# Hgrn2 attention and a balanced expert layer on one core: the first expert's tokens taken after the second digit of the capacity search

## The chip, the cores and the metric

The kernel runs on one core of a Trainium2 chip. The metric is the device time of one execution in microseconds (us); less is better. The engines go by short names: PE is TensorE (its weight loads are PEld), DVE is VectorE, ACT is ScalarE, POOL is GpSimd, SP is SyncE. PE accumulates in PSUM, eight banks of 128 x 512 float32.

## The reference

Inputs q, k, v, f_logit have the shape (4, 8, 768, 48). Per batch and head a 48 x 48 state decays by a gate and takes up one outer product a step; its product with q is the output y:

```python
f = 1.0 / (1.0 + np.exp(-f_logit))
for t in range(S):
    state = f[:, :, t, :, None] * state + np.einsum('bhd,bhe->bhde', k[:, :, t], v[:, :, t])
    y[:, :, t] = np.einsum('bhd,bhde->bhe', q[:, :, t], state)
```

The result, laid out as x of 3072 tokens by 384, goes to 8 experts of equal capacity, 384 tokens each. All (token, expert) logits x @ w_gate are taken in falling order; a pair is granted if its token is free and its expert not full. Each expert then computes relu(x @ w1) @ w2 with w1 384 x 1024 and w2 1024 x 384, all float32.

## The kernel before

**Attention** works on 24 chunks (6 stretches of 128 steps, 4 batches) in a pipeline whose stages are listed by hand. For each chunk the rows x and the logits are stored in a DRAM tile xd, 480 numbers a row: 384 of x and copies of the 8 logits. The last stores are issued from ACT (store, L374 to L377), since SP's queue takes the weights.

**Search** (L624 to L650). Every token first wants the expert of its largest logit. The margin at which the fullest expert has 384 takers is found digit by digit, four digits of five bits. For each digit DVE writes above (is a token over a threshold), 24 small products count by expert, DVE takes the largest count and compares it with the capacity, and a product with unit turns that into a new base in PSUM bank A[1]. Beside these steps PE turns the last three chunks (turn_y), ACT copies them to x, POOL adds the logits, ACT stores them. At the end come idle products (idle_turns, L105), which write to a bank that nobody reads.

**Lists** (fast(), L926 on). Tokens over the final base are sure of their expert. `positions` gives each its place in the expert's list by two products and a scan over nine kinds (no expert, and eight experts); `numbers` and `sort` turn that into tables of token numbers with 24 products. This is done twice with one in_line table: first for the two blocks of expert 0, then for all 30 blocks. From the token numbers POOL issues indirect DMAs, in this order in its queue: two whole tiles x of expert 0 (L793); the logits lg of up to 6 x 128 tokens that are not placed (L962); then xe, four quarter tiles a tile of tokens, two tiles for each of the experts 1 to 4 (L799).

**Experts.** A tile is 128 tokens. `turn` brings it to xeT: by PE products Xe and a copy on DVE and one on ACT for expert 0 (L716 to L720), by DVE block transposes for the rest (L727). `up` makes H by 24 products a tile or group of tiles, in three PSUM banks taken in turn (tags Y, Y, L), ACT writes relu(H) to hT (L741); `down` makes O by 8 products a tile (L751), ACT copies it to one of three buffers o (L756), and POOL issues the scatter to the output by token number (L757). A float32 product shows as two PE instructions in the profile.

**Rounds.** The tokens not placed go through seven rounds of a search of their own (search_rest, products cnt, L850) on DVE and PE, while PE works through the first two tiles of NA = 5 experts. `pe_work` is the list of PE pieces with their costs; `clock` holds an estimate of the time of PE and DVE, and `PE(cost)` issues pieces until PE's estimate has caught up, so the order of PE's queue is fixed when the kernel is built. When the rounds end, the third tiles of the five experts follow, then the last three experts with three tiles each.

**Weights.** Each expert has 3 MB. There are five slots. Experts 0 and 1 are loaded by SP once y0 of the last chunk is there; the next are issued from within the expert two places ahead (L744); experts 5 to 7 go to the slots 0 to 2, after the third tiles. A one-element copy into the new tile (L584) sets the moment at which the load may start.

If an expert of the first five has fewer than 256 sure tokens (few), or another check strikes, a general path computes all again.

Of the kernel before, what the change touches and what calls it, by code (L numbers as in the profile page):

```python
# [25 lines left out]
def kernel(  # L26
# [315 lines left out]
    def turn_y(G):  # L342
        G["X"] = X = lengthy if G["i"] + B == len(chunks) else T[0]
        for hp in range(HP):
            nc.tensor.transpose(out=X[:, 128 * hp:128 * hp + 128], in_=G["yT"][:, hp, :],  # L345
                                identity=ident[:])
# [72 lines left out]
    NL = 6  # L419
    NQ = NL + TE * E  # L420
    NA = 5
# [75 lines left out]
    notfirst = const([128, KC, NT], FP16, "notfirst")  # L497
# [81 lines left out]
    def load_weights(e, pool, slot, parts=(0, 1), behind=None):  # L579
        for part in parts:  # L580
            shape, src = (([128, DC, F], moe_w1), ([128, FC, D], moe_w2))[part]
            w = pool.tile(shape, FP32, name=f"w{part + 1}", tag=f"w{part + 1}_{slot}", bufs=1)
            if behind is not None:
                (nc.gpsimd.tensor_copy if e < 2 else nc.scalar.copy)(  # L584
                    out=w[:, 0, 0:1], in_=behind)
# [37 lines left out]
    def search(over, choice, n):  # L623
        base = A[1][:, 128:129]  # L624
        for d in range(DIGITS):
            r = counts["r"]
            if d:
                above, r = rt([n, TH], f"above{n}", FP16), Y[d % 2]
                for h in range(2):
                    part = slice(n * h // 2, n * (h + 1) // 2)  # L630
                    stt(above[:, part], last_of(over[:, part], TH), base,
                        mid_of(steps[d][:], n // 2), ALU.subtract, ALU.is_ge)
                if d == 1:
                    gated(chunks[-1])
                    added0(chunks[-1])
                elif d == 2:
                    last_codes()
                for go in (turn_y, copy_y, with_logits, store):
                    go(chunks[d - DIGITS])
                for c in range(n):  # L640
                    nc.tensor.matmul(out=r[0:TH, 0:E], lhsT=above[:, c, :],
                                     rhs=choice[:, c, :], start=(c == 0), stop=(c == n - 1))
            most, filled = rt([1], "most"), rt([1], "filled", FP16)
            reduce(most[0:TH], r[0:TH, 0:E], ALU.max)
            ts(filled[0:TH], most[0:TH], CAP - 0.5, ALU.is_ge)
            nc.tensor.matmul(out=base, lhsT=units[d][0:TH, :], rhs=filled[0:TH],
                             start=(d == 0), stop=(d == DIGITS - 1), skip_group_check=True)
        idle_turns(3, Y[DIGITS % 2])
        return base
    def load_gate():  # L650
        for r in range(2):
            for a in range(2):
                nc.sync.dma_start(
                    out=wg_rows[DP * r:DP * r + DH, 2 * a:2 * a + 2],
                    in_=moe_w_gate.rearrange(
                        "(a r b d) e -> a r d b e", a=2, r=2, b=2)[a, r])
# [4 lines left out]
    with tc.manual_schedule(engines=FIXED):  # L661
# [7 lines left out]
        for e in range(2):  # L669
            load_weights(e, early, e, behind=chunks[-1]["y0"][:, 0, 0:1])  # L670
        base = search(over0[:], choice0, NT)
# [4 lines left out]
    def fast():  # L676
        stack = ExitStack()
        turns = {"H": cycle("YYL"), "O": cycle("A"), "r": cycle("T"), "b": cycle(["small"])}

        def bank(name, tag):  # L680
            return ps(name, next(turns[tag]))

# [3 lines left out]
        pe_work = deque()  # L686
        clock = {"pe": 0.0, "dve": 0.0}

        def V(n=1, cost=0.21):
            clock["dve"] += n * cost  # L690

        def PE(cost):
            while pe_work and clock["pe"] < clock["dve"] + 0.1:
                piece()
            clock["pe"] = max(clock["pe"], clock["dve"] + 0.1) + cost
            clock["dve"] = max(clock["dve"], clock["pe"] + 0.22)

        def piece():
            cost, go = pe_work.popleft()
            go()  # L700
            clock["pe"] += cost

        tiles = iter(range(NT))

        def ffn(e, first_block, n, ahead=None):
# [5 lines left out]
            def turn(i):  # L711
                def by_matmul():
# [6 lines left out]
                    nc.vector.tensor_copy(out=xT[:, 0, 0:128], in_=X[0][:, 0:128])  # L719
                    nc.scalar.copy(out=xT[:, 1:DC, 0:128],  # L720
# [10 lines left out]
                return (0.65, by_matmul) if e == 0 and first_block < 2 else (0.0, by_blocks)  # L731

            def up(ft, d):
                def go():
# [5 lines left out]
                    if d == DC - 1:  # L740
                        nc.scalar.activation(out=hT[:, ft, 0:w], in_=L["H"][:, 0:w], func=AF.Relu)  # L741
                        if ahead is not None and ft in (1, 6):
                            load_weights(ahead, pools[ahead], ahead, (ft // 6,),
# [46 lines left out]
        def fetch(e, i):  # L790
            if e == 0 and i < 2:
# [74 lines left out]
        def positions(kind, nk, n, code, notfirst_, held):  # L866

            incl = rt([nk, n], f"incl{n}", FP16)
            P = bank("P", "r")
            w = nk * n  # L870
            Pv = P[:, 0:w].rearrange("p (k c) -> p k c", c=n)
            PE(0.1)
            nc.tensor.matmul(out=Pv, lhsT=after16[:], rhs=kind[:], start=True, stop=False)
            nc.vector.tensor_tensor_scan(incl[:].rearrange("p k c -> p (k c)"), notfirst_,
                                         kind[:].rearrange("p k c -> p (k c)"), 0.0,
                                         op0=ALU.mult, op1=ALU.add)
            V(cost=0.1 + w / 350)
            PE(0.2)
            nc.tensor.matmul(out=Pv, lhsT=ones16[:], rhs=incl[:], start=False, stop=held is None)
            if held is not None:  # L880
                nc.tensor.matmul(out=Pv, lhsT=ones16[:], rhs=last_of(held, n), start=False,
                                 stop=True)
            sums = P[:, 256:256 + nk]
            total = rt([nk], f"total{n}", FP16)
            nc.vector.tensor_copy(out=total[:], in_=incl[:, :, n - 1])
            own, pos = rt([nk, n], f"own{n}"), rt([n], f"pos{n}")
            tt(own[:], Pv, kind[:], ALU.mult)
            reduce(pos[:], own[:].rearrange("p k c -> p c k"), ALU.max)
            q, line, blk = rt([n], f"q{n}"), rt([n], f"line{n}", FP16), rt([n], f"blk{n}", FP16)
            ts(q[:], pos[:], 0.5 - 64.0, ALU.add, 1.0 / 128.0, ALU.mult)  # L890
            ts(q[:], q[:], 12582912.0, ALU.add, -12582912.0, ALU.add)
            stt(line[:], q[:], -128.0, pos[:], ALU.mult, ALU.add)
            tt(blk[:], q[:], code, ALU.add)
            V(9)
            return total, line, blk

# [29 lines left out]
        with tc.manual_schedule(engines=engines):  # L926
            code = rt([NT], "code", FP16)
            stt(code[:], over0[:], base, code0[:], ALU.is_ge, ALU.mult)
            kind = rt([KC, NT], "kind", FP16, 1)
            tt(kind[:], mid_of(code[:], KC), kinds[:], ALU.is_equal)  # L930
            total, line, blk = positions(kind, KC, NT, code[:],
                                         notfirst[:].rearrange("p k c -> p (k c)"), None)
            idle_turns(11, "A")
            p0 = place_of(0, 0)
            r, in_line = sort(line, numbers(blk, value[:], blocks[:, p0:p0 + 2], NT, 2), NT, 2, 4)
            idle_turns(6, "A")
# [582 lines left out]
```

## Time and profile before

| | |
|---|---|
| median of 3 runs | 432.75 us (431.65 to 433.54) |
| the profiled execution | 431.0 us |
| its span on the core | 429.2 us |
| mean granted PE clock | 0.982 |
| PE busy | 410.2 us, 96% |
| DVE, ACT, POOL busy | 207.2, 149.5, 175.1 us |
| HBM read, written | 48.91 MB, 10.62 MB |

How to read it: the profile is of one execution. The span is what its engines' records cover. Times in the timeline are microseconds from the start of the span. A matmul record's length holds its way through the array as well, so lengths of products that follow each other overlap; the pitch of a row of them is read from the distance between the first and the next thing. The attention ends at about 137, the search at about 147.5, the lists at about 158; H of expert 0 starts at 160.35; the first two tiles of five experts last until 277.6, the third tiles until 329.9, the three whole experts until 422.8.

### The profile page before, as it was taken

The numbers are of one execution on the slowest core, as the hardware profiler recorded it, in microseconds if no ns is written. First come the engines' busy times: TensorE is split into PE (matmuls) and PEld (weight loads), VectorE is DVE, ScalarE is ACT, GpSimd is POOL, SyncE is SP. The second block draws the span as 40 slices with busy tenths as digits, with TensorE's granted clock in tenths as the row PEclk, the third lists the DMA queues.
The fourth block names the chain that finished last, engine by engine and source line by source line (L and its number), as shares of the span: only waits on it lengthen the run. The fifth ranks groups of instructions, "written<-read, shape, count | busy, mean of one in ns | idle before, by whom it ended". The sixth has DMA issues, their size and how long they took to land.

```text
span 429.2 us, 11122 instructions
## 1 busy us (share of the span) xinstructions
PE 410.2 (96%) x4560; PEld 299.7 (70%) x4560; DVE 207.2 (48%) x713; ACT 149.5 (35%) x357; POOL 175.1 (41%) x308
## 2 busy tenths in 40 slices
PE   7899999999999889799999999999999999999993
PEld 3678888888878557777776768688886555555552
DVE  6589888888898750566766665200012202100000
ACT  3678777777774102211121212122222211201200
POOL 4344454444432037777501020775177727301001
PEclk9999999999999599899999999999999999999999
DMA  8899899989862987528372000169961202100001
GB/s 165 155 170 190 193 203 200 214 188 195 191 171 69 390 302 162 191 53 280 127 233 100 2 19 20 41 188 344 333 199 50 57 23 55 40 18 37 0 21 42
DMA packets 118509, 60.42 MB, mean 141 GB/s; under 512 B 103376, under 2 KB 114768, under 8 KB 117424
## 3 DMA queue, kind: packets, MB, share of 16 engines
q1 hardware_dynamic: 113344, 49.30, 43.4%
q0 software_dynamic: 4672, 9.57, 8.0%
q8 instruction: 38, 0.62, 0.6%
q10 hardware_dynamic: 432, 0.74, 0.4%
q14 instruction: 23, 0.19, 0.2%
HBM read 48.91 MB, written 10.62 MB: 139 GB/s over the span
## 4 chain that ended last, share of the span: by engine, by line
PE 61%; issue 19%; POOL 10%; DVE 5%; DMA 3%; ACT 1%; POOLq 0%; DVEq 0%
PE H L737 16%; PE O L751 15%; POOL xe L799 6%; PE T L235 5%; PE A L277 4%; PE L L172 4%; PE Y L307 3%; POOL out_dram L757 3%; PE L L362 2%; PE T L345 2%; PE small L256 2%; PE Y L318 2%; DMA lg<-xd,at_l 2%; PE small L200 2%; PE T L107 1%
## 5 line engine op out<-in xcount | busy, mean ns | idle before, releaser
L737 PE MATMUL H<-xeT,w 128*128 128x128 f32 (+2 forms) x672 | 134.1, 356 | 3.1 <-DVE xeT L719 3.1
L751 PE MATMUL O<-w,hT 128*128 128x384 f32 x384 | 128.9, 489 | 0.0
L737 PEld LDWEIGHTS H<-xeT,w 128*128 128x128 f32 x672 | 102.7, 194 | 29.1 <-DVE xeT L719 3.9
L751 PEld LDWEIGHTS O<-w,hT 128*128 128x128 f32 x384 | 71.3, 190 | 44.7
L799 POOL DMA_INDIRECT xe<-xd,quad x88 | 83.4, 948 | 36.2 <-issue 25.9
L741 ACT ACTIVATE hT<-H 128x128 f32<-128x128 f32 (+2 forms) x112 | 39.6, 354 | 92.4 <-PE H L737 91.1
L757 POOL DMA_INDIRECT out_dram<-o,tok x24 | 23.5, 981 | 115.5 <-ACT o L756 112.5
L727 DVE STREAM_TRANSPOSE xeT<-xe 128x96 f32<-128x96 f32 x88 | 22.4, 288 | 85.0 <-DMA xe<-xd,quad 59.6
L756 ACT COPY o<-O 128x384 f32<-128x384 f32 x24 | 11.5, 479 | 117.6 <-PE O L751 107.6
L285 DVE COPY_PREDICATED am<-mask,A 128x512 f32<-128x512 int32 x48 | 34.5, 724 | 0.2 <-PE A L277 0.2
L210 POOL TENSOR_TENSOR gl<-span,spans 128x4 f32<-128x4 f32 x20 | 3.9, 197 | 50.6 <-PE Y L307 26.8
L277 PE MATMUL A<-qT,kT 48*64 48x128 f32 (+1 forms) x768 | 22.3, 251 | 0.4 <-ACT kT L243 0.3
L172 PE MATMUL L<-g,wcum 128*128 128x384 f32 x48 | 19.7, 491 | 1.0 <-ACT g L168 1.0
L158 POOL COPY w<-v 64x256 f32<-64x256 f32 x48 | 18.9, 395 | 2.5
L307 PE MATMUL Y<-am,v 64*64 64x64 f32 (+1 forms) x368 | 19.8, 243 | 0.0
L277 PEld LDWEIGHTS A<-qT,kT 48*64 48x64 f32 x768 | 18.7, 133 | 1.4 <-ACT kT L243 0.5
L307 PE MATMUL Y<-am,w 64*64 64x128 f32 (+1 forms) x368 | 19.2, 243 | 0.0
L177 DVE TENSOR_SCALAR dl<-L 128x384 f32<-128x384 f32 x24 | 13.3, 556 | 10.0 <-PE L L172 9.6
L307 PEld LDWEIGHTS Y<-am,v 64*64 64x64 f32 x368 | 17.9, 134 | 0.0
L235 PE MATMUL T<-ident,qg 128*128 128x128 f32 x96 | 15.8, 286 | 2.0 <-DVE qg L188 2.0
L307 PEld LDWEIGHTS Y<-am,w 64*64 64x64 f32 x368 | 17.3, 134 | 0.0
L345 PEld LDWEIGHTS T<-ident,yT 128*128 128x128 f32 x92 | 11.6, 147 | 8.0 <-ACT qT L243 4.3
(245 smaller groups left out, 528.8 us busy)
## 6 DMA issues: line engine op xcount, KB each, us to landing
w<-in_moe_w_dram SPq DMA_DIRECT2D x16, 1536.0 KB, 9.2
xd<-x SPq DMA_DIRECT2D x21, 240.0 KB, 3.2
f<-in_f_logit_dram SPq DMA_DIRECT2D x24, 192.0 KB, 4.2
k<-in_k_dram SPq DMA_DIRECT2D x24, 192.0 KB, 4.8
q<-in_q_dram SPq DMA_DIRECT2D x24, 192.0 KB, 4.4
v<-in_v_dram SPq DMA_DIRECT2D x24, 192.0 KB, 4.6
xe<-xd,quad POOLq DMA_INDIRECT x88, 2.5
xd<-x ACTq DMA_DIRECT2D x3, 240.0 KB, 7.7
```

The costliest lines, as they stand in the source:

```text
L172: nc.tensor.matmul(out=G["Lv"], lhsT=wcum[:], rhs=g_bufs[G["i"] % NB][:, :, 0:DH], start=True, stop=True)
L235: nc.tensor.transpose(out=t[:, 128 * hp:128 * hp + 128], in_=G[src][:, 2 * hp:2 * hp + 2, :].rearrange("t h d -> t (h d)"), identity=ident[:])
L277: nc.tensor.matmul(out=A[par][to, 128 * hp + first * j:128 * hp + 128], lhsT=G["kT"][rows, hp, HC * j:HC * j + HC], rhs=G["qT"][rows, hp, ...
L285: nc.vector.copy_predicated(am[:, par].rearrange("s (a b) t -> s a b t", b=2), mask[:].unsqueeze(2).to_broadcast((128, 2, 2, 128)), A[par] ...
L307: nc.tensor.matmul(out=G["Y"][r0][DP * r:DP * r + DP, 128 * blk + first:128 * blk + 128], lhsT=v, rhs=G["am"][rows, h % 2, h // 2, first:128],
L345: nc.tensor.transpose(out=X[:, 128 * hp:128 * hp + 128], in_=G["yT"][:, hp, :], identity=ident[:])
L727: nc.vector.transpose(out=xT[:, :, 128 * i + 32 * g:128 * i + 32 * g + 32], in_=x[:, g])
L737: nc.tensor.matmul(out=L["H"][:, 0:w], lhsT=slots[e][0][:, d, 128 * ft:128 * ft + 128], rhs=xT[:, d, 0:w], start=(d == 0), stop=(d == DC - 1))
L741: nc.scalar.activation(out=hT[:, ft, 0:w], in_=L["H"][:, 0:w], func=AF.Relu)
L751: nc.tensor.matmul(out=L["O"][:, 0:D], lhsT=hT[:, ft, 128 * i:128 * i + 128], rhs=slots[e][1][:, ft, :], start=(ft == 0), stop=(ft == FC - 1))
L757: nc.gpsimd.indirect_dma_start(out=outs[next(tiles)][:, :], out_offset=bass.IndirectOffsetOnAxis(ap=token(e, first_block + i), axis=0), in ...
L799: nc.gpsimd.indirect_dma_start(out=t[:, PW * g:PW * g + PW], out_offset=None, in_=xd[:, :].rearrange("n (a x) -> (n a) x", x=PW), in_offse ...
```

## The change

- NA goes from 5 to 6, with five slots as before (NS): a sixth expert, number 5, takes part with its first two tiles, in slot 0, whose weights are loaded within expert 4. Expert 0 so loses its weights before its third tile; they are loaded again into slot 2, and its third tile is the last work of the kernel. Order of third tiles: 5, 1, 2, 3, 4; then experts 6 and 7 whole; then expert 0's third.
- The search is cut into `digit_of`. After digit two, tokens whose first choice is expert 0 and that lie one step of that digit over the base are taken as sure (first_over, kind[:, KC]). They get places at once by `positions` with one kind, and the two first tiles come from them.
- Digits three and four, and the code of all tokens, are placed behind the issue of expert 0's gathers. The other lists come after that, with ten kinds (expert 0's tokens of the early list, and those that became sure later, which start behind the early ones by held_c), between the first pieces of H and O. Their in_line table is made anew.
- Expert 0's weights alone are loaded early, and only when x of the last chunk is there; expert 1's are issued within expert 0, and so on, one expert ahead.
- Expert 1's two tiles come like expert 0's, as whole rows x and by PE products; the copies are on DVE for tile (0,0) alone and on ACT for the other three. POOL's queue now has two x, then two x of expert 1, six lg, 24 xe (experts 2 to 4), then the scatters; expert 5's gathers stand behind expert 2's scatters.
- The idle products: 5, 4, 3 and 3 (all on bank A[0]) in place of 3, 11, 6, 6 and 6. In the order of the instructions in the built kernel the first five stand inside the search: one ahead of the first product with unit, two ahead of the counts of digit two, two between their halves. Behind the product with unit of digit two come the turn of chunk -2 (four products), the two products of `positions`, the turn of chunk -1, and the tokens products.
- The turned chunks -2 and -1 have banks of their own (lengthy, small).

The core of the diff:

```diff
     def turn_y(G):
-        G["X"] = X = lengthy if G["i"] + B == len(chunks) else T[0]
+        G["X"] = X = (small if G["i"] + 1 == len(chunks) else
+                      lengthy if G["i"] + 2 == len(chunks) else T[0])
...
-    NA = 5
+    NA, NS = 6, 5
...
-                (nc.gpsimd.tensor_copy if e < 2 else nc.scalar.copy)(
+                (nc.scalar.copy if e else nc.gpsimd.tensor_copy)(
                     out=w[:, 0, 0:1], in_=behind)
...
-        for e in range(2):
-            load_weights(e, early, e, behind=chunks[-1]["y0"][:, 0, 0:1])
-        base = search(over0[:], choice0, NT)
+        digit_of(0, over0[:], choice0, NT)
+        digit_of(1, over0[:], choice0, NT, [
+            lambda: gated(chunks[-1]), lambda: added0(chunks[-1]),
+            lambda: stt(first_over[:], over0[:], 0.0, choice0[:, :, 0], ALU.max, ALU.mult),
+            *turned_and_stored(-3)])
+        for go in turned_and_stored(-2):
+            go()
+        kind = route.tile([128, KC + 1, NT], FP16, name="kind", tag="kind", bufs=1)
+        base = A[1][:, 128:129]
+        stt(kind[:, KC], first_over[:], base, steps[1][:, 0:1].to_broadcast((128, NT)),
+            ALU.subtract, ALU.is_ge)
+        total_c, line_c, blk_c = positions(kind[:, KC:KC + 1], 1, NT, None,
+                                           notfirst[:, 0], None, first=T[1])
+        for go in turned_and_stored(-1):
+            go()
+        load_weights(0, early, 0, behind=chunks[-1]["x"][:, 0:1])
...
-                    nc.vector.tensor_copy(out=xT[:, 0, 0:128], in_=X[0][:, 0:128])
+                    copy = nc.scalar.copy if e or first_block else nc.vector.tensor_copy
+                    copy(out=xT[:, 0, 128 * i:128 * i + 128], in_=X[0][:, 0:128])
...
-                return (0.65, by_matmul) if e == 0 and first_block < 2 else (0.0, by_blocks)
+                return (0.65, by_matmul) if e < 2 and first_block < 2 else (0.0, by_blocks)
...
-            total, line, blk = positions(kind, KC, NT, code[:],
-                                         notfirst[:].rearrange("p k c -> p (k c)"), None)
-            idle_turns(11, "A")
+            idle_turns(5, A[0])
             p0 = place_of(0, 0)
-            r, in_line = sort(line, numbers(blk, value[:], blocks[:, p0:p0 + 2], NT, 2), NT, 2, 4)
-            idle_turns(6, "A")
+            r, _ = sort(line_c, numbers(blk_c, value[:], blocks[:, p0:p0 + 2], NT, 2), NT, 2, 4)
...
             for i in range(2):
                 lists[0, i] = tok0[:, i:i + 1]
                 fetch(0, i)
-            r, _ = sort(line, numbers(blk, value[:], blocks[:], NT, NQ), NT, NQ, 12, in_line)
+            idle_turns(4, A[0])
+            digit_of(2, over0[:], choice0, NT, [last_codes])
+            idle_turns(3, A[0])
+            digit_of(3, over0[:], choice0, NT)
+            idle_turns(3, A[0])
+            code = rt([NT], "code", FP16)
+            stt(code[:], over0[:], base, code0[:], ALU.is_ge, ALU.mult)
+            clock.update(pe=1.0, dve=0.0)
+            for e in range(NA):
+                ahead = e + 1 if e + 1 < NA else None
+                if e:
+                    add(ffn(e, 0, 2, ahead))
+                    if e == 2:
+                        for i in range(2):
+                            pe_work.append((0.0, lambda i=i: fetch(NS, i)))
+                else:
+                    add(ffn(e, 0, 1, ahead))
+                    add(ffn(e, 1, 1))
+            for _ in range(5):
+                piece()
+            tt(kind[:, 0:KC], mid_of(code[:], KC), kinds[:], ALU.is_equal)
+            tt(kind[:, 1], kind[:, 1], kind[:, KC], ALU.subtract)
+            nc.vector.tensor_copy(out=held_c[:, 1:2], in_=total_c[:])
+            V(4)
+            total, line, blk = positions(kind, KC + 1, NT, code[:],
+                                         notfirst[:].rearrange("p k c -> p (k c)"), held_c[:])
+            tt(total[:, 1:2], total[:, 1:2], total[:, KC:KC + 1], ALU.add)
+            r, _ = sort(line, numbers(blk, value[:], blocks[:], NT, NQ), NT, NQ, 4)
...
+            for i in range(2):
+                fetch(1, i)
             lg = rt([NL, E], "lg", FP32, 1)
...
-            for e in range(1, NA):
+            for e in range(2, NS):
                 for i in range(2):
                     fetch(e, i)
-            clock.update(pe=4.0, dve=0.0)
...
-            clock["dve"] = 14.0
+            V(46)
+            PE(0.1)
...
-            for e in range(NA):
+            slot = {NS: 0, NA: 0, NA + 1: 1, 0: 2}
+            for e, new in ((NS, NA), (1, NA + 1), (2, 0), (3, None), (4, None)):
                 fetch(e, 2)
                 add(ffn(e, 2, 1))
-                if NA + e < E:
-                    pe_work.append((0.0, lambda e=e: load_weights(NA + e, pools[e], e)))
-            for e in range(NA, E):
-                for i in range(TE):
+                if new is not None:
+                    pe_work.append((0.0, lambda e=new: load_weights(e, pools[slot[e]], slot[e])))
+            for e, first in ((NA, 0), (NA + 1, 0), (0, 2)):
+                for i in range(first, TE):
```

## The prediction

> **What bounds the kernel now.** I read the page's first two parts, then the timeline around the hand-over from the search to the experts, then TensorE's waits. PE is busy for 96% of the span. From its first H product to the end it has one hole:
>
> ```profile
> PE 410.2 (96%) x4560; PEld 299.7 (70%) x4560; DVE 207.2 (48%) x713; ACT 149.5 (35%) x357; POOL 175.1 (41%) x308
> ```
> ```profile
> 153.81 0.17 DVE L429 TENSOR_SCALAR tok<-found 128x2 int32<-128x2 f32 x1
> ...
> 155.68 1.19 POOL L793 DMA_INDIRECT x<-xd,tok  x1 [13.27 <-DVE numb L425]
> ...
> 160.35 3.64 PE L737 MATMUL H<-xeT,w 128*128 128x128 f32 x30 [0.21 <-DVE xeT L719]
> ```
> ```profile
> 172.29 0.31 DVE L429 TENSOR_SCALAR lg<-lg,low_scale 128x48 f32<-128x48 f32 x1 [7.29 <-DMA lg<-xd,at_l]
> ...
> 174.22 0.28 DVE L719 COPY xeT<-Xe 128x128 f32<-128x128 f32 x1
> ...
> 174.56 0.76 PE L737 MATMUL H<-xeT,w 128*128 128x128 f32 x4 [2.93 <-DVE xeT L719]
> ```
>
> Columns: start, length, engine, line, operation; in brackets the idle time before it and what ended it. The token numbers (tok) are there at 153.98, the gather starts at 155.68, H at 160.35. The hole is at 174.56: DVE waits for the lg gather, and the copy of tile (0,1) stands behind that wait. After it PE never waits; the last product ends at 422.8, and 6.4 us of copy, scatter and end follow. So the time is (start of H) + (PE's work and holes) + 6.4.
>
> The hole costs more than itself. By stretch (the column before the last two is PE's granted clock):
>
> ```profile
> 174.00:175.00 1.00, 0.44 (x4) 0.44 (x5) 0.50 (x3) 0.00 (x0) 0.69 (x2) 1.00 1.04 393
> 175.00:176.00 1.00, 1.00 (x12) 0.98 (x11) 0.43 (x2) 0.00 (x0) 0.70 (x2) 0.54 0.99 363
> 176.00:177.00 1.00, 1.00 (x7) 1.00 (x7) 0.90 (x4) 0.28 (x1) 0.92 (x1) 0.50 0.59 193
> 177.00:178.00 1.00, 1.00 (x6) 1.00 (x6) 0.05 (x1) 0.28 (x1) 0.77 (x1) 0.50 0.24 52
> 178.00:179.00 1.00, 1.00 (x13) 0.94 (x12) 0.18 (x1) 0.28 (x1) 0.69 (x2) 0.75 0.20 37
> ```
>
> After 2.9 us without work the clock is halved for 3.4 us: 0.46+0.5+0.5+0.25 = 1.7 us lost. From the pieces, 174.56 to 188.03 lasts 13.5 for work of 11.3, so about 2.1. I take 5.0 for hole and clock.
>
> **PE's work, old and new.** From the chain: H of 128 tokens 0.223 a product (48 half passes in 5.36), of 256 0.447, of 384 0.645; O 0.645. A pair of tiles is then 21.05, a tile alone 10.52, a triple 30.96. Old: 2 x 10.52 + 4 x 21.05 + 5 x 10.52 + 3 x 30.96 = 250.7; with Xe 0.5, m 0.15, the rounds' small products 6.2 (pairs 1 to 4 take 89.6 for 84.2, and 0.8 in the first) and the hole 5.0 it is 262.5, against 262.4 measured. New: 3 x 10.52 + 5 x 21.05 + 5 x 10.52 + 2 x 30.96 = 251.3. Xe is now three times inside, 1.5 (expert 1 is turned on PE too). The other lists move into this stretch: 24 token products 1.5 (155.03 row), three P products of 0.17 and quad 0.25 make 2.3. With m and rounds that is 261.5: **0.9 less** than before, since the hole's 5.0 pays for the rest.
>
> Is that hole gone? The copy of (0,1) is now on ACT. In the built order the first cnt stands behind 24 + 24 + 4 H, 16 O, four turned tiles less one and the lists, 26.8 us after H starts. By DVE's rows the lists take to 11.6 (below), two x and six lg gathers at 1.25 each reach 21, landing 2.4, DVE 2.0: 25.4. It fits, by 1.4.
>
> **Start of H.** Digits follow each other by 2.3 to 2.4 (products with unit at 140.28, 142.58, 144.94, 147.30). Two leave the path: 4.7. One kind for nine: own and pos (0.38 + 0.63) become one product of 24 elements, 0.2; code and kind (0.5) one of 0.25: 1.0. Added: first_over 0.25, which lies beside PE. In the built order the five idle products of the list stage stand inside the search: one ahead of the first unit product, two ahead of and two inside digit two's counts; and the turn of chunk -2 stands ahead of the product on the new kind. At half clock (as the rows of 141 to 151 show; idle products 0.37, a turn 1.1) the unit product comes at 144.1, P at 145.7, tok at 149.7. At full clock (0.27, 0.65): 148.4. The gather also needs the last store. It is issued at 147.2 or 145.4; the three last stores now run before weights, not behind them. The two rows:
>
> ```profile
> xd<-x SPq DMA_DIRECT2D x21, 240.0 KB, 3.2
> ...
> xd<-x ACTq DMA_DIRECT2D x3, 240.0 KB, 7.7
> ```
>
> I take 3.5, near the first, since the store is issued ahead of its only rival: landed 150.7 or 148.9; the gather a little under 1 us later (155.68 against 146.75 + 7.8) and 3.4 to 3.8 to land. But the weights of expert 0 start at 147.6 now, and two such loads needed 10 us before (138.0 to 148), so a gather held till they drain lands at 157.4. Beside it run digits three and four, 5.0 from tok, then three idle products: Xe not before 155.5 or 154.0. From Xe to H 0.8. H starts at 154.7 to 158.2; I take **156.6, 3.75 earlier**. The first weights, issued at 147.6, land by 155 (7.2 before).
>
> **The new wait.** GpSimd's queue is strict. Before, six lg and 32 xe gathers run at 1.25 each, then the first scatter:
>
> ```profile
> 204.73 0.94 POOL L799 DMA_INDIRECT xe<-xd,quad  x1 [0.30 <-issue]
> 205.97 1.01 POOL L757 DMA_INDIRECT out_dram<-o,tok  x1 [0.30 <-issue]
> ```
> ```profile
> 210.27 0.48 ACT L756 COPY o<-O 128x384 f32<-128x384 f32 x1 [4.92 <-PE O L751]
> ```
> ```profile
> 298.52 0.48 ACT L756 COPY o<-O 128x384 f32<-128x384 f32 x1 [5.07 <-DMA out_dram<-o,tok]
> ```
>
> o has three buffers, so the fourth copy (210.27) needs the first scatter landed (205.97 + 2.5 = 208.5): 1.8 us of slack. That such a wait holds ACT is seen once, at 298.52. In the new order the first issue waits for the lists: H starts, PE reaches the last tokens product at 11.1 (24 H, P, Xe, 5 O), DVE gives tok at 11.6, GpSimd starts at 12.0. Then 2 x, 6 lg and 24 xe: 32 x 1.25 = 40, so the first scatter is issued 52.2 after H's start (45.6 before) and lands at 54.7. The fourth o is ready on PE at 25.2 + 22.3 = 47.5. ACT stands 7.2 us, and behind it the hT of expert 2. PE still has the three H banks, nine products of 0.447 and small ones, until 51.7; ACT needs 0.9 for o and the first hT, so PE goes on at 55.7: **a hole of 4.0**. With a half clock after it, 1.4 (of 1.7 at most, as it depends on where the hole falls), 5.4 in all. Price bounds: 0 if the scatters get through, 7 if the lists come 1.5 us late.
>
> The Trainium skill, "TensorE: Matmul & The Clock Gate", section "Why this matters for your kernels", asks for no idle gap above about 3 us, with the clock halved after one idle window. Its figure would have let the 2.93 us gap pass, which the rows above show halved; for the new hole both say halved. Its section on the clock gate lets the default be the slow clock, which speaks against taking idle products out: the rows of 141 to 151 fit that.
>
> At nothing: the ninth load of weights (3 MB) lies under 40 us of PE work, as the three late loads do now; the extra gather code beside PE; the ACT copies of expert 1, on an engine busy 35%.
>
> **Sum.** -3.75 (start) - 0.9 (work, old hole gone) + 5.4 (new hole) = +0.75; 0.2 for late pieces: **+0.95**. The profiled execution took 431.0 (span 429.2), so 431.95; the median of the runs is 432.75, and carried to it the forecast is **433.7**.
>
> **Rivals.**
> (1) No new hole: the scatters come in time or ACT is not held. For it: the slack of 1.8 before shows that GpSimd's order worked out there. Against: 32 issues at a pitch that never varied, and three buffers. Then -3.75 - 0.9 = -4.65: 428.1.
> (2) Slower: H starts late and cold. Fifteen idle products stand where 32 were. If the clock is halved at about 141, as before, nothing dense enough raises it (it came back at 151.2, only after a stretch with 14 idle products, 3.37 us busy of 3.40), the gather waits for expert 0's weights, H starts at 158.2 and its first 3.4 us run at half speed: -2.15 + 1.7 + 5.4 - 0.9 = +4.05: 436.8. It decides the sign once H starts after 157.2 and cold.
> (3) The tokens sure at the second digit are too few: the check sends everything through the general path, a multiple of the time.
>
> **How the numbers follow.** New hole 0.54, no hole 0.28, late and cold 0.17, general path 0.01. The first alone spreads from 431.5 to 436 (start 154.7 to 157.5, hole 3 to 5). Within 0.5% (2.2 us, about what a measurement of this kernel can tell): first 0.36, rival one 0.03, so 0.39. Faster: 0.25 from rival one, 0.03 from the first: 0.28. Slower: 0.15 + 0.17 + 0.01 = 0.33. The range takes in rival one's 428.1 and rival two's 436.8: 427.5 to 437.0.
>
> **What will show it.** Start of H (156.6) and its clock; tok near 149; no PE idle from then to the first cnt; ACT's fourth o waiting for out_dram about 7 us, PE idle 4 us some 52 us after H's start, and half clock behind it. A PE without that hole proves rival one; a hole at the first cnt means that lg was late.

## The result, and the profile after

The changed kernel takes **434.75 us** (median of 9 runs, 434.24 to 437.51) against 432.75 for the kernel before (9 runs, 430.24 to 433.81): a ratio of 1.0068, 95% interval 1.0040 to 1.0095, **0.7% slower**. The forecast was 433.7. The profiled execution of the changed kernel took 436.54 (span 434.7), 1.8 above its median, while that of before took 431.0, 1.75 below its own; so the two traces differ by 5.5 us where the medians differ by 2.0. Part of that has nothing to do with the change: ACT's first copy of yT after 20 us stands at 21.58 in the one and 20.72 in the other, the last of the attention at 138.07 and 137.06. The changed kernel's execution thus entered the changed code 1.0 late, and where it matters I take this off.

The page's first part: PE is busy for a smaller share, though it has more to do.

```profile
PE 413.9 (95%) x4600; PEld 306.5 (71%) x4600; DVE 208.6 (48%) x721; ACT 152.7 (35%) x374; POOL 170.4 (39%) x300
...
xd<-x ACTq DMA_DIRECT2D x3, 240.0 KB, 2.0
```

The second line is the last three stores: landed in 2.0 where they took 7.7. The timeline at the hand-over from the search to the experts (start, length, engine, line, operation, idle time before and its releaser):

```profile
149.56 0.17 DVE L430 TENSOR_SCALAR tok<-found 128x2 int32<-128x2 f32 x1
150.77 1.19 POOL L844 DMA_INDIRECT x<-xd,tok  x1 [2.43 <-DVE above L433]
...
156.93 0.89 PE L766 MATMUL Xe<-ident,x 128*128 128x128 f32 x3 [1.52 <-issue]
...
157.77 2.20 PE L788 MATMUL H<-xeT,w 128*128 128x128 f32 x8
```

The first tokens are there 4.2 us earlier than before (5.2 with the late entry taken off) and the gather is issued 4.9 earlier, but from its issue to Xe pass 6.2 us (3.9 before), and H starts at 157.77: 2.6 earlier, 3.6 with the late entry taken off. Eight records of H last 2.20, where at full clock 48 last 5.36. The stretches (the last three columns are PE's granted clock, the DMA share and GB/s) show it cold (at half clock) until 163.1:

```profile
162.00:163.00 1.00, 1.00 (x7) 0.89 (x7) 0.00 (x0) 0.28 (x1) 0.00 (x0) 0.50 0.87 172
163.00:164.00 1.00, 1.00 (x10) 1.00 (x10) 0.79 (x2) 0.28 (x1) 0.00 (x0) 0.91 0.53 197
```

The old hole, at the first cnt, is gone: lg is used at 184.53, the first cnt follows, and PE waited for neither.

```profile
184.53 0.31 DVE L430 TENSOR_SCALAR lg<-lg,low_scale 128x48 f32<-128x48 f32 x1 [9.41 <-DMA lg<-xd,at_l]
...
186.78 0.31 PE L901 MATMUL cnt<-above_r,in_line 128*128 128x32 f16 x6
```

The new hole, in order of time: the last of 32 gathers, the first scatter behind it, the fourth o on ACT, and PE's next H, which needed ACT's hT. ACT stood idle for 12.43 us ahead of that copy; PE's products of this O ended at 207.70, so 7.5 of them were the wait for the scatter.

```profile
211.30 0.94 POOL L850 DMA_INDIRECT xe<-xd,quad  x1 [0.30 <-issue]
212.55 1.01 POOL L808 DMA_INDIRECT out_dram<-o,tok  x1 [0.31 <-issue]
```
```profile
215.25 0.48 ACT L807 COPY o<-O 128x384 f32<-128x384 f32 x1 [12.43 <-DMA out_dram<-o,tok]
```
```profile
216.07 4.64 PE L788 MATMUL H<-xeT,w 128*128 128x256 f32 x10 [4.11 <-ACT hT L792]
```

Ten records of H last 4.64 there, where twelve took 2.84 ahead of the hole. The stretches: idle, then half clock until 221.

```profile
213.00:214.00 1.00, 0.00 (x0) 0.00 (x0) 0.00 (x0) 0.00 (x0) 0.69 (x2) 1.00 0.14 28
...
218.00:219.00 1.00, 1.00 (x4) 0.82 (x3) 0.00 (x0) 0.00 (x0) 0.00 (x0) 0.50 0.65 160
...
221.00:222.00 1.00, 1.00 (x5) 0.86 (x5) 0.86 (x5) 0.34 (x1) 0.00 (x0) 0.90 0.87 369
```

The last products:

```profile
422.81 5.33 PE L802 MATMUL O<-w,hT 128*128 128x384 f32 x16
```

From H's start to their end pass 428.14 - 157.77 = 270.4 us; the prediction's work of 261.5 with a hole of 5.4 makes 266.9. Between the two stand the cold start of H (2.7: half of 157.77 to 163.1) and a loss to the clock behind the hole of 2.5 (half of 216.07 to 221) in place of 1.4, together 3.8, less 0.3 for all the rest.

### The profile page after: what moved, and what is told of

The parts are those of the page before. It is cut to its first block, busy times and chain, and to the rows that moved or that the text cites. A ratio compares the mean times of both kernels' runs of the same rounds, so it can differ in the third digit from the quotient of the medians.

```text
span 434.7 us, 11230 instructions
## 1 busy us (share of the span) xinstructions
PE 413.9 (95%) x4600; PEld 306.5 (71%) x4600; DVE 208.6 (48%) x721; ACT 152.7 (35%) x374; POOL 170.4 (39%) x300
## 4 chain that ended last, share of the span: by engine, by line
PE 61%; issue 17%; POOL 11%; DMA 5%; DVE 4%; ACT 1%; POOLq 0%; DVEq 0%; ACTq 0%
PE H L788 15%; PE O L802 14%; POOL xe L850 8%; PE T L235 5%; PE A L277 4%; DMA xe<-xd,quad 4%; PE L L172 4%; PE Y L307 3%; POOL out_dram L808 2%; PE L L363 2%; PE T L346 2%; PE small L256 2%; PE Y L318 2%; PE small L200 2%; PE T L107 1%
## 5 line engine op out<-in xcount | busy, mean ns | idle before, releaser
L788 PE MATMUL H<-xeT,w 128*128 128x128 f32 (+2 forms) x720 | 138.6, 349 | 4.1 <-ACT hT L792 4.1
L788 PEld LDWEIGHTS H<-xeT,w 128*128 128x128 f32 x720 | 110.2, 197 | 25.8 <-ACT hT L792 4.5
L850 POOL DMA_INDIRECT xe<-xd,quad x80 | 75.9, 949 | 24.6 <-issue 21.3
L792 ACT ACTIVATE hT<-H 128x128 f32<-128x128 f32 (+2 forms) x120 | 40.8, 341 | 88.1 <-PE H L788 86.9
L778 DVE STREAM_TRANSPOSE xeT<-xe 128x96 f32<-128x96 f32 x80 | 19.7, 287 | 94.9 <-DMA xe<-xd,quad 59.7
L430 DVE TENSOR_SCALAR full_r<-cnt,there 128x32 f32<-128x32 f32 x24 | 6.0, 251 | 25.5 <-PE cnt L901 25.5
```

Of the source, the lines that this page charges most:

```text
L778: nc.vector.transpose(out=xT[:, :, 128 * i + 32 * g:128 * i + 32 * g + 32], in_=x[:, g])
L788: nc.tensor.matmul(out=L["H"][:, 0:w], lhsT=slots[e][0][:, d, 128 * ft:128 * ft + 128], rhs=xT[:, d, 0:w], start=(d == 0), stop=(d == DC - 1))
L850: nc.gpsimd.indirect_dma_start(out=t[:, PW * g:PW * g + PW], out_offset=None, in_=xd[:, :].rearrange("n (a x) -> (n a) x", x=PW), in_offse ...
```

## The experiments

The experiments are called e1 to e12. Each time is a median, each ratio one to the kernel before, run beside it on the same chip (431.46 beside e1, e2, e4 and e5; 432.39 beside e3, e6, e7 and e8; 432.41 beside e9 to e11). Start times are those of one profiled execution each.

**Is the hole the wait of the fourth o, and is it GpSimd's order?** First (e1), a fourth buffer:

```diff
-  o = work.tile([128, D], FP32, name="o", tag="o", bufs=3)
+  o = work.tile([128, D], FP32, name="o", tag="o", bufs=4)
-  t = rows[e, i] = work.tile([128, D], FP32, name="xe", tag="xe", bufs=7)
+  t = rows[e, i] = work.tile([128, D], FP32, name="xe", tag="xe", bufs=6)
```

> The changed kernel with four o buffers instead of three, paid for by the seventh xe buffer (xe 7 to 6; o and xe are both 128 x 384 f32). Theory (the new hole is the wait of the fourth o copy for the first scatter, which stands behind 32 gathers on GpSimd): the fifth o is the first to need the first scatter; it is ready about 16 us after the fourth, past the scatter's landing. ACT's wait of 12.43 us on out_dram at 215.25 and PE's 4.11 us at 216.07 are gone, and so is the half clock behind them (about 2.2): 6 us less, 428.5 to 429.5. Rival (PE would wait there anyway, for a gather or for the rounds' small products, or the half clock moves elsewhere): the hole comes back within 20 us and the time stays above 433. Six xe buffers instead of seven should hold up nothing before expert 5's gathers: six tiles are fetched first, and expert 5's stand behind expert 2's products; if they do, DVE's turns of expert 5 come late and PE waits there.

Measured: 430.76, ratio 0.9973 (0.9953 to 0.9994). The scatter is as late as before, the fourth o no longer waits for it, and PE has no wait between Xe and the end:

```profile
206.96 0.48 ACT L807 COPY o<-O 128x384 f32<-128x384 f32 x1 [4.92 <-PE O L802]
211.78 1.01 POOL L808 DMA_INDIRECT out_dram<-o,tok  x1 [0.30 <-ACT hT L792]
```

Second (e2), three buffers, and eight gathers fewer ahead of the scatter:

```diff
-                    if e == 2:
+                    if e in (1, 2):
                         for i in range(2):
-                            pe_work.append((0.0, lambda i=i: fetch(NS, i)))
+                            pe_work.append((0.0, lambda e=e, i=i: fetch(e + 3, i)))
...
-            for e in range(2, NS):
+            for e in range(2, NS - 1):
                 for i in range(2):
                     fetch(e, i)
```

> The changed kernel with the eight gathers of expert 4 moved on GpSimd's queue: they are issued behind expert 1's products (as expert 5's are behind expert 2's) and so behind the first scatters; three o buffers stay. Theory (place in the queue): 24 issues at 1.25 us instead of 32 stand ahead of the first scatter, which comes 10 us earlier, 44.8 us after the start of H instead of 54.8, landed at 47.5, about when the fourth o is ready: hole and half clock gone or under 1 us, 428.5 to 429.5, the same as with a fourth buffer. Rival (the buffers, or something that both share, not the queue): with three buffers the wait stays, time above 433. Expert 4's gathers then are issued about 45 to 60 us after the start of H, and expert 4 is needed some 100 us after it: no wait there.

Measured: 429.30, ratio 0.9938 (0.9914 to 0.9963), and again no wait of PE. Now the scatter goes first, and the same fourth o finds its buffer free:

```profile
202.19 1.01 POOL L808 DMA_INDIRECT out_dram<-o,tok  x1 [0.30 <-issue]
...
207.37 0.48 ACT L807 COPY o<-O 128x384 f32<-128x384 f32 x1 [4.92 <-PE O L802]
```

Both cures work, by different means, so the cause is shown: the scatters' place on GpSimd's queue with three buffers. In ratios the hole with its clock is worth 0.95% (4.1 us) by e1 and 1.3% (5.6 us) by e2; forecast were 5.4. What e1 lacks to e2 is left open; their intervals overlap.

**What holds the first gather?** Expert 0's weights behind y0 instead of the last x (e5):

```diff
         attention(-1, ALL)
+        load_weights(0, early, 0, behind=chunks[-1]["y0"][:, 0, 0:1])
...
-        load_weights(0, early, 0, behind=chunks[-1]["x"][:, 0:1])
```

> The changed kernel with the weights of expert 0 loaded behind y0, before the digits, as the kernel before did for two experts, instead of behind the last x. Theory (the first gather is slowed by the 3 MB of weights that drain beside it: 6.1 us against 3.8 before): the weights are landed before the gather is issued, the gather takes under 4 us, PE's idle 1.5 us ahead of the first Xe goes, and H starts about 1.5 earlier, at 156.3 in the profiled execution's time: 433.0 to 433.5. Price that may take it back: the last stores now drain beside the weights (2.0 us to land now, 7.7 in the kernel before) and the gather waits for them. Rival (stores late): the gather is issued 2 to 4 us later, H starts no earlier or up to 2 us later, 435 to 437. The hole at the fourth o stays in both, moved with H.

Measured: 436.23, ratio 1.0085 (1.0057 to 1.0113): the rival. The stores, beside the weights, land in 5.7, and the gather is issued 2.5 later; Xe starts at 157.00, where it was 156.93 without the edit. The gather itself did get shorter, as the theory had it: 3.7 from its issue to Xe, where it was 6.2.

```profile
153.27 1.19 POOL L844 DMA_INDIRECT x<-xd,tok  x1 [9.65 <-DVE above L433]
```
```profile
xd<-x ACTq DMA_DIRECT2D x3, 240.0 KB, 5.7
```

So 3 MB of weights in one piece slow either the stores or the gather. Half early, half behind the gather (e6, with e2's edit; so are e3, e7 and e8 below):

```diff
         attention(-1, ALL)
+        load_weights(0, early, 0, (0,), chunks[-1]["y0"][:, 0, 0:1])
...
-        load_weights(0, early, 0, behind=chunks[-1]["x"][:, 0:1])
...
                 fetch(0, i)
+            load_weights(0, early, 0, (1,), rows[0, 0][:, 0:1])
```

> The kernel of e2 (expert 4's gathers later), with the first half of expert 0's weights (w1) loaded behind y0, before the digits, and the second half (w2) behind the first gathered tile, so that neither the last stores nor the gather of tile (0,0) have a load of weights beside them. Theory (H starts late because the one gather shares the DMA engines with 3 MB of weights, and loading both early only moves the weights beside the stores): the last store lands in about 2, the gather is issued at 150.5 as in e2 and takes 3 to 4 instead of 6.5; x is there at 154, Xe follows the third idle product of the last digit at 155.2, H starts at 156.0 instead of 158.2, and the clock comes back one window of 3.4 earlier: 2.2 + 0.7 less than e2, 426.4. Rival (the gather's own length, or w2 arriving late for the first O): H at 157.5 or later, or a wait of PE ahead of the first O: 429 or more.

Measured: 427.49, ratio 0.9880 (0.9834 to 0.9926), 0.6% below e2's, though the two intervals just overlap. The gather has landed by 154.3 and H starts at 156.08 for the 156.0 that was expected, though this execution entered the changed code 1.3 later than that of the kernel before:

```profile
150.86 1.19 POOL L844 DMA_INDIRECT x<-xd,tok  x1 [7.05 <-DVE above L433]
...
154.34 0.19 POOL L585 COPY w<-x 128x1 f32<-128x1 f32 x1 [0.84 <-DMA x<-xd,tok]
155.28 0.85 PE L766 MATMUL Xe<-ident,x 128*128 128x128 f32 x3
156.08 2.16 PE L788 MATMUL H<-xeT,w 128*128 128x128 f32 x8
```

**The cold start.** Idle products moved to where PE stood still ahead of the tokens (e7):

```diff
         for go in turned_and_stored(-1):
             go()
+        idle_turns(4, A[0])
...
-            idle_turns(5, A[0])
...
                     nc.tensor.matmul(out=r[:, 0:nq], lhsT=in_line[:, c // 2, :, c % 2],
                                      rhs=numb[:, :, c], start=(c == 0), stop=(c == n - 1))
+                if nq == 2 and c0 + part < n // 2:
+                    idle_turns(1, A[0])
```

> The kernel of e2, with the idle products in other places: the five that stand inside the first two digits go, four stand between the turn of the last chunk and the token products, and one behind each of the first two groups of token products. PE was idle there 1.1, 0.23 and 0.23 us. Theory (cold start: H runs 3.8 us at half clock because no window since 141.5 was full): tok comes 0.2 to 0.5 later by the idle products, but a window ending near 151.7 is full, the clock comes back, and H starts at full clock: 1.9 less minus 0.3: 427.7. Rival one (PE's wait of 2.2 for x before Xe halves the clock again, as the hole of 2.93 did): no gain, 429 to 430. Rival two (idle products only lengthen the path): 430 to 431.

Measured: 428.46, ratio 0.9908 (0.9874 to 0.9942). The clock comes back at 150.3 as the theory says, and is halved again from 153.7, as the first rival says: PE then waits 2.9 us for x, H starts at 158.70, cold until 164 (this execution took 430.52, 2.1 above the median). The median is 0.3% below e2's by ratio, within the intervals: no gain is shown. Second (e3), eight idle products instead of three behind the last digit:

```diff
             digit_of(3, over0[:], choice0, NT)
-            idle_turns(3, A[0])
+            idle_turns(8, A[0])
```

> The kernel of e2, with eight idle products instead of three behind the last digit, where PE waits 2.2 us for the first Xe. Theory (cold start): five more of 0.37 fill 1.85 of the 2.24 idle, the window of 155.2 to 158.6 is then nearly full, and the clock comes back at 158.6 instead of 162.0; H starts at the same 158.2 and loses 0.2 instead of 1.9: 1.7 less, 427.6. Rival (the window isn't full enough, or H is held by something else): within 0.5 of 429.3.

Measured: 429.06, ratio 0.9930 (0.9904 to 0.9955), against 0.9938 for e2. In the profiled execution (428.17) PE no longer waits for Xe and the clock is back at 159.7, 1.7 after H starts; but the runs go from 427.43 to 431.03, and the median shows no gain. Neither edit alone brings a gain that can be measured.

**Do the two add?** e6 and e7 together (e9), then with one idle product behind the counts of the third and fourth digit (e10):

```diff
+        if d > 1:
+            idle_turns(1, A[0])
         most, filled = rt([1], "most"), rt([1], "filled", FP16)
```

> The edits of e2 (expert 4's gathers later), e6 (weights of expert 0 split) and e7 (idle products pinned ahead of and between the token products) together. Theory (two causes that add: a gather held by weights, and a cold start): x is there at 154 as in e6 and H starts at 155.8; the clock comes back at about 150.4 as in e7 and falls again at about 153.8 (the last digits leave PE a quarter idle), but the window from 153.8 is full of H and it is back at 157.2 instead of 160.2: 1.5 less than e6, ratio to the kernel before 0.9845 (e6 0.988). Rival (the two overlap: one gain hides the other): 0.987 to 0.989.

> The kernel of e9 with one more idle product behind the counts of the third digit and one behind those of the fourth, where PE waits 0.42 us for DVE's filled. Theory: with full windows the clock doesn't fall at 153.8, H starts at full clock: 0.7 less than e9, ratio 0.983. Rival (the fall comes from something else, or the idle product delays the unit product): the clock falls as in e9, 0.9845 or a little more.

Measured: e9 425.77, ratio 0.9850 (0.9826 to 0.9875); e10 425.71, ratio 0.9854 (0.9829 to 0.9878). Both **beat both kernels**, in ratios by 1.5% the one before and by 2% the change. e9 comes to the theory's 0.9845 rather than the rival's 0.987 to 0.989, but its interval still meets e6's, so the gain over e6 is not shown. H starts at 155.02 in e10 and is cold only to 156.1:

```profile
155.02 1.70 PE L791 MATMUL H<-xeT,w 128*128 128x128 f32 x8
```

But the extra idle products of e10 did not hold the clock, and e10 is no faster than e9, as its rival has it: the clock falls at 152.7, 3.4 us after it came back at 149.3, though PE was 81 to 100% busy in between:

```profile
150.00:151.00 1.00, 0.81 (x15) 0.55 (x14) 0.78 (x6) 0.00 (x0) 1.00 (x1) 1.00 0.00 0
151.00:152.00 1.00, 0.89 (x12) 0.42 (x12) 0.87 (x2) 0.00 (x0) 0.70 (x2) 1.00 0.24 52
152.00:153.00 1.00, 0.94 (x23) 0.62 (x20) 0.42 (x3) 0.00 (x0) 0.56 (x1) 0.84 0.61 194
```

**What was the old hole worth, and who pays for its going?** Two edits of the change in the kernel before (e4):

```diff
-                    nc.vector.tensor_copy(out=xT[:, 0, 0:128], in_=X[0][:, 0:128])
+                    copy = nc.scalar.copy if first_block else nc.vector.tensor_copy
+                    copy(out=xT[:, 0, 0:128], in_=X[0][:, 0:128])
...
-            clock["dve"] = 14.0
+            clock["dve"] = 20.0
```

> The kernel before, with only two small edits that the change also has in its way: the copy of Xe's first piece of tile (0,1) by ACT instead of DVE, and the rounds' first cnt put 6 us later in PE's order. It prices the term of the sum that took the old hole of 2.93 us with its half clock at 5.0. Theory: the hole at 174.56 is gone, and the half clock of 175.0 to 178.5 with it, less what a fourth o that is ready 5 us earlier now waits for the first scatter (1.8 us of slack in the kernel before, so ACT waits about 3 us, PE under 1): 4 to 5 less, 427.8 to 428.8. Rival one (the half clock isn't due to the hole): 2.9 less, 429.8. Rival two (the time of before is set elsewhere, the rounds' end or the third tiles): within 1 us of 432.75.

Measured: 432.02, ratio 1.0021 (0.9989 to 1.0052). Rival two: no gain is shown. The hole at 174 is gone, and PE waits for the first third tile, whose gathers stand behind the rounds (the granted clock stays at 1.00 behind this wait):

```profile
276.31 5.62 PE L738 MATMUL H<-xeT,w 128*128 128x128 f32 x48 [2.98 <-DVE xeT L728]
```

The counterpart (e8): e2 without the sixth expert ahead of the rounds' end.

```diff
-    NA, NS = 6, 5
+    NA, NS = 5, 5
...
-            for e, new in ((NS, NA), (1, NA + 1), (2, 0), (3, None), (4, None)):
+            for e, new in ((0, 5), (1, 6), (2, 7), (3, None), (4, None)):
...
-            for e, first in ((NA, 0), (NA + 1, 0), (0, 2)):
+            for e, first in ((5, 0), (6, 0), (7, 0)):
```

> The kernel of e2 without the sixth expert's first two tiles ahead of the rounds' end: five experts with two tiles first, then the five third tiles, then three experts whole, as the kernel before has it; all 24 tiles are still computed. Theory (the earlier start of H and the dropped hole only pay because the sixth expert covers the rounds): PE runs out of first tiles at about 272, while the first third tile's gathers can't be issued before 276.7 and x is turned at 282: a hole of 9 to 10 us with half clock behind it, 439 to 441. It would also say why the old hole's 5.0 could not be had alone in e4, where PE waited 2.98 for the first third tile. Rival (the rounds end sooner without the sixth expert's products between them, or the sixth expert's cover isn't needed): under 432.

Measured: 439.93, ratio 1.0176 (1.0128 to 1.0224), as the theory had it, with a hole of 7.68 and half clock behind it (48 products in 7.96 instead of 5.4):

```profile
283.56 7.96 PE L788 MATMUL H<-xeT,w 128*128 128x128 f32 x48 [7.68 <-DVE xeT L778]
```

So the sixth expert is worth about 10 us to e2 (2.4% by ratio). Last (e11), everything but the early first tiles, on the kernel before: e4's edits, the sixth expert with its third tiles and weights as in the change, and expert 4's gathers later.

```diff
-    NA = 5
+    NA, NS = 6, 5
...
-            for e in range(1, NA):
+            for e in range(1, NS - 1):
                 for i in range(2):
                     fetch(e, i)
...
+                    if e in (1, 2):
+                        for i in range(2):
+                            pe_work.append((0.0, lambda e=e, i=i: fetch(e + 3, i)))
```

> The kernel before with all four digits ahead of the first tokens as it was, and with only the later parts of the change: a sixth expert in the first slot and its order of third tiles and weights, the two edits of e4 that take the old hole away, and expert 4's gathers later as in e2. It tells what the early first tiles themselves bring. Theory (the start of H is 2.2 earlier in e2 than in the kernel before, and 1.9 of it goes back as half clock, so the gain of e2 over the kernel before comes from the old hole, which the sixth expert's cover lets go): no hole, 4 to 5 less than the kernel before, ratio 0.989 to 0.991, about that of e2 (0.9938) or better. Rival (the early tiles carry the gain): 0.996 or more.

Measured: 427.76, ratio 0.9897 (0.9869 to 0.9925), as the theory had it, with no hole and H at full clock:

```profile
160.58 3.64 PE L738 MATMUL H<-xeT,w 128*128 128x128 f32 x30 [0.21 <-DVE xeT L720]
```

With all its digits ahead of the first tokens it is no slower than e2 (0.9938): as built, the early tiles bring nothing that can be measured. With the weights split and the idle products moved (e9 and e10) they bring 2.0, or 0.5% (425.77 and 425.71 against 427.76 on the same chip).

The twelfth (e12) puts expert 4's gathers back among the 32 (the edit of e2 undone in e11):

> The kernel of e11, with expert 4's eight gathers back among the 32 that are issued one after another ahead of the first scatter. Theory (the hole at the fourth o is made by the place of the lists: in the change GpSimd's first gather for expert 1 comes 14.8 us after the start of H, in the kernel before 2 us ahead of it): the 32 gathers and six lg run from about 158 to 206, the first scatter is landed at about 208.7 while the fourth o is ready at 205.3, so ACT waits some 3 us, PE under 1: within 1.5 of e11, ratio 0.990 to 0.993. Rival (32 gathers ahead of the scatters make the hole wherever the lists stand): PE idle 3 us or more with half clock behind it, 5 more than e11, ratio 1.000 or above.

Inconclusive: it ran on a chip where it and the kernel before took far longer (494.0 and 500.04, ratio 0.9860 with 0.9823 to 0.9897), with waits of PE that no other run has, up to 16.6 us ahead of Xe. The fourth o came at 244.74 there, long after the first scatter at 214.61, so this run does not test the question. But e4 does. It has the lists ahead of H, three o buffers, and six lg and all 32 xe gathers ahead of the first scatter, and without the old hole its fourth o does wait for that scatter:

```profile
209.10 0.48 ACT L757 COPY o<-O 128x384 f32<-128x384 f32 x1 [8.35 <-DMA out_dram<-o,tok]
```

PE's products of this O ended at 205.54, so ACT was held for 3.5 us (the theory of e12 said some 3), and PE did not wait at all. With the lists beside H it is 7.5 and 4.11. So 32 gathers ahead of the scatters do not by themselves open a hole in PE's work. The first scatter is issued 45.6 after H's start in e4 and 54.8 in the change, whose lists come later; the two kernels differ in more than that, though, so that the lists' place alone does it is likely and not shown.

## Why the prediction was right, and where its sizes were off

The time (434.75 for 433.7) and the mechanism of the likeliest case were right: a new hole outweighs the earlier start. That the number came so near is in part luck, since one error hid another and a cost was left out. The interval of the measured ratio, 1.7 to 4.1 us more, does not hold the forecast of 0.95 more. By its steps:

- **The new hole.** Place, cause and length were right: PE idle 4.11 for 4.0, ACT held 7.5 for 7.2, and e1 and e2 take it away. The scatter was issued 54.8 after H's start for 52.2 and the fourth o was ready at 49.9 for 47.5, both later by about what the cold H cost. The loss to the clock behind it was 2.5 in the trace for 1.4, since the fall came at 214.4, in the hole, and the return only at 221. By medians hole and clock together are 4.1 to 5.6 for 5.4.
- **The start of H.** Right in sum, 156.8 with the late entry taken off for 156.6, by two errors that cancel: at half clock I had tok at 149.7 and, with stores of 3.5, the gather at about 151.6; in that reckoning they came at 148.7 and 149.8, and the gather, which I let land in 3.4 to 3.8, took 6.2 to Xe. I had the other end (a gather held till the weights drain, H at 158.2) and took a value between. e5 and e6 show that the weights do it (3.7 to Xe with them ahead of the gather, 3.5 to its landing with half of them ahead and half behind). The stores took 2.0, and the gather's lag behind them, read as a little under 1 us, is 1.1 by the figures given. The profiled executions of e1, e2 and e8, whose code is the same up to there, have H at 157.5 to 157.7 with the late entry taken off, so 156.6 was early by 0.2 to 1.1.
- **The cold H** is the step that failed. I had half clock at the start of H only in rival two, as part of a late start, at a price of 1.7; it came with a start that was not late, and cost 2.7 in the profiled execution, and 1.9 in that of e2, which is e2's median run (429.30). It is a term of the likeliest case, not a rival of it.
- **Sum and median.** Forecast +0.95; with 2.7 of cold H, 1.1 more behind the hole, 0.2 of start and 0.3 less for the rest it is +4.6, and the profiled executions differ by 4.5 without the late entry. The medians differ by 2.0 only. The profiled one is no measure of the sum: its mean granted clock is 0.966, where the five of the nine that took 434.2 to 434.8 had 0.971 to 0.978 (one at 0.971 took 437.5, so the clock isn't all of it). How much of the cold H a median run has was not profiled.
- **PE's work and the old hole.** Right: e2, whose last products start at 415.60 and last 5.33, has 420.93 - 158.16 = 262.8 from H's start to their end with 1.9 of cold start, 260.9 for a forecast of 261.5. The old hole is not just hidden by the cold H: in e10, cold for 1.1 us, PE waits 0.24 at the first cnt. That the old hole's 5.0 can be had is shown by e11 (4.65 less than before, with the sixth expert and the later gathers) and that it needs the sixth expert by e4 and e8. The prediction had the sixth expert only as another order of the same work, and did not see that the hole's going hangs on it.
- **Rival one** (no new hole, 4.65 less) describes e2 once the cold start is added: 4.65 less 1.9 is 2.75, and e2's ratio is 0.62% or 2.7 us below 1. The change just does not have that order. Rival two's lateness and cold came in part, its sum (436.8) did not.

The page cited in the prediction, the Trainium skill's "TensorE: Matmul & The Clock Gate", lets the default be the slow clock in its section "Part 1: The HAM clock gate": the cold start agrees, with half clock from 142.7 to 163.1 in the changed kernel.

## What to carry to other kernels

Moving work earlier can delay whatever stands behind it in an engine's queue: after the lists went beside H, GpSimd's gathers ran later against PE, and a scatter at their tail held an o buffer, ACT and PE in turn. Follow every moved step's DMA issues to the buffers that they free, and ask of a regained hole whether the next stage has work to fill it (e4: nothing; e11, with a sixth expert and the later gathers, 4.65 us). An early start at half clock, fed by a gather that runs beside the weights, brought nothing that could be measured until both were mended (e2 against e9 and e10).

## What the runs showed of the hardware that was not expected

- The length of a gap alone does not decide the granted clock. PE's gap of 2.93 in the kernel before was followed by half clock, its gap of 2.98 in e4 was not. And the clock falls without any long gap: in e10 at 152.7 after 3.4 us in which PE was 81 to 100% busy with idle products and counts 8 columns wide, whereas the kernel before kept full clock through a sparser stretch:

```profile
152.00:153.00 1.00, 0.72 (x16) 0.55 (x16) 1.00 (x2) 0.00 (x0) 0.00 (x0) 1.00 0.91 371
153.00:154.00 1.00, 0.79 (x12) 0.60 (x13) 0.50 (x4) 0.00 (x0) 0.00 (x0) 1.00 1.04 396
154.00:155.00 1.00, 0.57 (x4) 0.22 (x3) 0.94 (x2) 0.00 (x0) 0.00 (x0) 1.00 1.06 400
```

  So PE's busy share in the profile does not decide it alone. What does stays open.
- A gather of 128 rows issued beside 3 MB of weight loads took 6.2 us from issue to Xe in the changed kernel, and 3.7 in e5 with the weights ahead of it. The last three stores of 240 KB took 2.0 (the median of the three) with the weights behind them, 3.3 beside half of the weights (e6), and 5.7 (e5) or 7.7 (the kernel before) beside all that was loaded early.
